# Row maxima of attention: half of the first two key blocks as a relu of differences on ScalarE and one fused add-and-maximum on VectorE

## The chip, the cores and the metric

The kernel runs on one NeuronCore of a Trainium2 chip. Its engines are TensorE (PE in the profile, with its weight loads PEld), VectorE (DVE), ScalarE (ACT), GpSimd (POOL) and SyncE (SP, which only issues DMAs here). The metric is the device time of one execution in microseconds; lower is better. Every engine works through its own instructions in order and waits on semaphores of the others.

## The reference

One transformer block on 2048 rows of width 576, in fp32: a LayerNorm with scale and shift made from a condition `c`, attention with 32 heads of 18 columns, a residual with a gate, a second modulated LayerNorm, and a gated MLP of width 4608.

```python
mod = (_silu(c) @ w_mod).reshape(c.shape[0], 6, 1, -1)
sa, ca, ga, sb, cb, gb = (mod[:, 0], mod[:, 1], mod[:, 2], mod[:, 3], mod[:, 4], mod[:, 5])
h = _layernorm(x, axis=-1) * (1 + ca) + sa
x = x + ga * _A_ref(h, A_wqkv, A_wo)
...
    scores = jnp.einsum("bhqd,bhkd->bhqk", q, k) * scale
    p = _softmax(scores, axis=-1)
    o = jnp.einsum("bhqk,bhkd->bhqd", p, v)
```

The part that matters here is the softmax over 2048 keys, and in it the maximum of each row of scores, which is subtracted before the exponential.

## The kernel before

**Stages.** A first stage makes the modulation, the LayerNorm, and q, k and v; q and k are written to HBM (`qk`) transposed, each as a high part (rounded to PE's fp32r format) and a low part. Then comes attention, and beside its later units the output projection, the second LayerNorm and the operands of the MLP; the MLP follows.

**Units.** Attention runs over 32 units. A unit is one half of the queries (1024) with two heads: units 0 to 15 are the sixteen pairs of heads with the first half, units 16 to 31 the same pairs with the second half. `load_heads(u)` brings a unit's q and k from HBM with eight DMAs on SP's queue, two units ahead; head 0 lies in partitions 0 to 63 and head 1 in 64 to 127, so that matmuls of the two heads lie in different rows of PE. Each head has 54 rows of operands (high times high, high times low, low times high) and two more rows for the negated maximum.

**Maxima.** `maxima()` is a generator that works one unit ahead of the exponentials. A unit has 64 of its turns: for each of 8 query tiles of 128 rows, 4 key blocks of 512 and 2 heads (the head changes fastest, then the key block), one matmul into a PSUM bank (L411) and one VectorE reduce that takes the maximum of the bank's 512 columns into a column of `mx` (L415). At the end of a unit a small reduce (L421) gives the negated maximum `nm` of each row; `spread()` transposes it on PE, splits it into a high and a low part (`mrows`) and sends these by DMA into the spare rows of q. That way the exponentials' matmul subtracts the maximum by itself.

**Steps.** A unit has 16 steps, one per block of 128 keys. In a step, four score matmuls with the keys on the partitions (L877) each give a bank of 128 x 512, each followed by one exponential on ScalarE (L881), and `values()` multiplies the exponentials of two steps earlier with v (L501, eight instructions, in four column groups of PE). The order of PE's instructions is written out by hand: `STEPS` gives one string for even and one for odd steps, where `t` is a score matmul, `m` a turn of the maxima, `v` the values and `w` a place for other work (transposes of outputs and maxima, and in later units a piece of the output projection or of the second LayerNorm). The two steps together make PE's order values, six matmuls, values, ten matmuls. The other engines' order is decided by a scheduler. Maxima are 24 turns and more ahead of the steps, so that the first `m` of a unit is turn 25 of the next unit, that is query tile 3, key block 0, head 1; the eight turns of a query tile thus begin with the last matmul of the group of ten (head 0) and the first one of the group of six (head 1).

**Banks.** `bank()` (L80) hands out seven PSUM banks in turn to maxima, scores and transposes alike; a matmul waits until the bank that was given out seven calls before has been read. The eighth bank, `o`, takes the values of a unit; at its end ScalarE copies it to SBUF (`taken()`, L515), PE transposes it, VectorE takes the reciprocal of the row sums (L529), ScalarE copies the transposed output (L540) and GpSimd scales it (L544).

**Before attention.** `project_qk` multiplies weights and LayerNorm output (L267); ScalarE rounds the high part (L273), VectorE subtracts the low one (L274), and SP's DMA writes them out (L279). In its last part, seven tiles of weights alternate with the first turns of the maxima (`run`). `key_set` sets the spare rows of the key buffers to 1 (L367).

```python
STEPS = "vtmmttmvtm", "tmttwmtmm"
```

Of the kernel before, what the change touches and what calls it, by code (L numbers as in the profile page):

```python
# [15 lines left out]
F32 = mybir.dt.float32  # L16
F32R = mybir.dt.float32r
AF = mybir.ActivationFunctionType
ALU = mybir.AluOpType
# [13 lines left out]
DM = 512  # L33
HALF = D // 2
EPS = 1e-5
SCALE = float(DH) ** -0.5
HW = S // 2
UNITS = H
# [13 lines left out]
def tile_block(ctx, tc, x_in, wqkv, wo, w_gate, w_up, w_down, c_in, w_mod, out):  # L52
# [23 lines left out]
    sc_b = early.tile([P, 5, 32], F32, name="sc_b")  # L76
# [27 lines left out]
    def modulate(row, wm, pieces, takes):  # L104

        pm = bank()
        for parts in pieces:
            for t in range(5):  # L110
                k = ksize(t)
                for v in range(2):
                    for g, to, f0, n in parts:
                        q = 32 * (2 * v + g)
                        nc.tensor.matmul(
                            pm[q : q + 32, to : to + n], sc_b[:k, t, :],
                            wm[t][:k, v * D + f0 : v * D + f0 + n],
                            start=t == 0, stop=t == 4, tile_position=(0, q),
                        )
# [12 lines left out]
        for b in range(3):  # L132
            nc.tensor.transpose(pt[:, b * P : (b + 1) * P], row[:, b * P : (b + 1) * P], ident)
        cols = pt[:, 0:384].rearrange("p (b q) -> p b q", q=P)
        for v, (dst, add) in enumerate(takes):
            if add is None:
                for g in range(2):
                    q = 64 * v + 32 * g
                    nc.sync.dma_start(gates[v : v + 1, g * HALF : (g + 1) * HALF], row[q : q + 1, 0:HALF])
                nc.sync.dma_start(dst, gates[v : v + 1, :].to_broadcast([P, D]))  # L140
            else:
                n = dst.shape[-1]
                nc.vector.tensor_scalar_add(dst[:, 0:3], cols[:, :, 64 * v], add)
                nc.vector.tensor_scalar_add(dst[:, 3:n], cols[:, 0 : n - 3, 64 * v + 32], add)
# [89 lines left out]
    qk = dram.tile([2, 2, D, S], F32R, name="qk")  # L234
# [24 lines left out]
    def project_qk(both, ahead=None):  # L259

        pl = stage.tile([P, 2, 1024], F32R, name="pl")
        for i, ((parts, wh, wl), ch) in enumerate(both):
            acc = bank()
            cols = slice(ch * 512, (ch + 1) * 512)
            ts_ = terms(wh, wl, slice(0, P))
            for n, (w, t) in enumerate(ts_):
                nc.tensor.matmul(  # L267
                    acc, w, hT[:, t, cols], start=n == 0, stop=n == len(ts_) - 1
                )
            if ahead:  # L270
# [3 lines left out]
            nc.vector.tensor_sub(lo, acc, hi.bitcast(F32))  # L274
        for i, ((parts, wh, wl), ch) in enumerate(both):
            p0 = 0
            for col, n in parts:
                which, f0 = col // D, col % D
                nc.sync.dma_start(  # L279
                    qk[which, :, f0 : f0 + n, ch * 512 : (ch + 1) * 512]  # L280
                    .rearrange("l f n -> f l n").bitcast(F32),
                    pl[p0 : p0 + n, :, i * 512 : (i + 1) * 512].bitcast(F32),
                )
                p0 += n

    def load_v(pool, hf):
        raw = pool.tile([P, 5, HALF], F32, name="wv_raw")
# [24 lines left out]
    with tc.tile_pool(name="ln", bufs=2) as ln:  # L312
# [6 lines left out]
        nc.vector.tensor_copy(sc_b, sc.unsqueeze(2).to_broadcast([P, 5, 32]))  # L319

        def normalized(ch):
            xs = []
# [13 lines left out]
        with tc.tile_pool(name="wmp", bufs=1) as wmp:  # L336
            zs = normalized(0)
            wm = wmp.tile([P, 5, 2 * D], F32, name="wm")
            wm = load_mod(wm[:, 0:4, :], wm[:, 4, :], 0)
            modulate(wmp.tile([P, 384], F32, name="mrow"), wm, QUARTERS, [(mcol[:, 1, :], 0.0), (mcol[:, 0, :], 1.0)])  # L340
        nc.gpsimd.memset(vaug, 1.0)
        wts = [load_qk([(0, P)]), load_qk([(D, P)])]
        with tc.tile_pool(name="wv0", bufs=1) as wvp:
            wv = load_v(wvp, 0)
            ln_transpose(ln, zs, hT, 0)
            zs = normalized(1)
            for ch in range(NCH):
# [17 lines left out]
    def key_set(t):  # L365
        for q in (32, 96):
            nc.gpsimd.memset(t[q : q + 32].bitcast(F32), 1.0)  # L367
        return t[:, 0:S]

    ksets = [key_set(temp([P, S], F32R)) for _ in range(2)]  # L370

# [3 lines left out]
    def load_heads(u):  # L375


        qs, ks = heads(u)
        half, p = divmod(u, H // 2)
        own = slice(half * HW, (half + 1) * HW)  # L380
        for h in range(2):
            rows = slice((2 * p + h) * DH, (2 * p + h + 1) * DH)
            two, one = (slice(64 * h + a, 64 * h + b) for a, b in ((0, 2 * DH), (2 * DH, 3 * DH)))
            nc.sync.dma_start(
                qs[two, :].bitcast(F32), qk[0, :, rows, own].rearrange("l f n -> f l n").bitcast(F32)
            )
            nc.sync.dma_start(qs[one, :].bitcast(F32), qk[0, 0, rows, own].bitcast(F32))
# [4 lines left out]
            nc.sync.dma_start(ks[one, :].bitcast(F32), qk[1, 1, rows, :].bitcast(F32))  # L392

    def maxima():

# [2 lines left out]
        last = None  # L398
        for u in range(UNITS):
            qs, ks = heads(u)  # L400
            mx = small.tile([P, 2 * n, 4], F32, name="mx")
            for i in range(8 * n):
                if last is not None and i == (9 if u == 1 else 8):
                    if u == 1:
                        spread(*last)
                    else:
                        state["spread"] = last
                qt, kc, h = i // 8, i // 2 % 4, i % 2
                rows = slice(64 * h, 64 * h + 3 * DH)
                sp = bank()  # L410
                nc.tensor.matmul(  # L411
                    sp, qs[rows, qt * P : (qt + 1) * P],
                    ks[rows, kc * 512 : (kc + 1) * 512], start=True, stop=True,
                )
                nc.vector.tensor_reduce(  # L415
                    mx[:, h * n + qt, kc : kc + 1], sp, axis=AX.X, op=ALU.max
                )
# [12 lines left out]
    def spread(qs, nm):  # L430
# [4 lines left out]
        parts = [small.tile([2 * n, P], F32R, name=f"mrows{l}", bufs=1) for l in range(2)]  # L435
        nc.scalar.copy(parts[0], tp)
        nc.vector.tensor_sub(parts[1], tp, parts[0].bitcast(F32))
        for h in range(2):
# [79 lines left out]
    def outputs():  # L518
# [9 lines left out]
        rec = epool.tile([P, 4, 4], F32, name="rec")  # L528
        nc.vector.reciprocal(rec, tq[:, :, :, DH])  # L529
        if half == 1 and p == H // 2 - 1:  # L530
            state["last"] = epool.tile([P, 8, 2 * DH], F32, name="last")
# [313 lines left out]
    for u in range(UNITS):  # L845
# [6 lines left out]
        for kt in range(NT):  # L852
# [31 lines left out]
            if u in (1, 3):  # L884
                if kt == 2:
# [4 lines left out]
                    row = slots.tile([P, 2560], F32, name="w1")[:, 0:384]  # L890
# [340 lines left out]
```

## Time and profile before

| | before |
|---|---|
| median of three runs | 2932.17 us (2931.83 to 2936.15) |
| span of the profiled execution | 2934.3 us |
| first exponential of attention | 234.76 us from the span's start |
| last exponential ends | near 1598 us |
| PE busy | 2867.2 us (98%) |
| VectorE busy | 2305.1 us (79%) |
| ScalarE busy | 1497.6 us (51%) |
| GpSimd busy | 614.7 us (21%) |

The profile is of one execution. The page gives the span of the program's instructions, and no other time of that execution. Its second part shows the busy share of each engine in 40 slices of 73 us; the fourth to the twenty-second are attention. A group's row holds the line, the engine, the operation, what it writes and reads, the shape, then busy time in us, mean ns of one, and the idle time of the engine just before, with what ended it. In a timeline each row has its start and length in us, with "xN" where instructions in a row are put together, and in brackets the idle time ahead of it. Neighbouring instructions of an engine overlap by some tens of nanoseconds, so that the distance from start to start is shorter than the mean duration. Ends of matmuls are modelled, so "busy" on PE takes in time in which it streams nothing.

### The profile page before, as it was taken

How to read it: one execution, taken by the hardware profiler on the slowest of the kernel's cores; microseconds unless marked ns; L12 is line 12 of the kernel's file. 1: busy time of each engine (PE TensorE's matmuls, PEld its weight loads, DVE VectorE, ACT ScalarE, POOL GpSimd, SP SyncE). 2: the span in 40 equal slices, each digit the busy share in tenths (PEclk: the TensorE clock that was granted, in tenths of full speed). 3: DMA queues.
4: the chain of work that ended last, by engine and by line, in shares of the span. 5: the costliest groups of instructions: out<-in, count | busy, mean ns of one | idle time of the engine just before them, and what ended most of it. 6: DMA issues, size and time to landing. Idle time of an engine off the chain costs nothing.

```text
span 2934.3 us, 46129 instructions
## 1 busy us (share of the span) xinstructions
PE 2867.2 (98%) x17141; PEld 1884.6 (64%) x17141; DVE 2305.1 (79%) x4021; ACT 1497.6 (51%) x2779; POOL 614.7 (21%) x793
## 2 busy tenths in 40 slices
PE   7999999999999999999999999998999999999999
PEld 6974333333334443443443788887888888888888
DVE  7278999999999999999992778888777555555555
ACT  3217778888887678878778333333332111111111
POOL 2001024444213110661102222233221100000000
PEclk9999999999999999999999999999999999999999
DMA  5333113333212110221125866686556854444443
GB/s 170 119 138 115 63 58 134 126 116 112 83 50 70 31 50 19 95 92 60 48 78 185 280 217 231 232 278 242 204 201 225 303 177 168 166 168 169 158 158 137
DMA packets 136089, 420.25 MB, mean 143 GB/s; under 512 B 18805, under 2 KB 56441, under 8 KB 123577
## 3 DMA queue, kind: packets, MB, share of 16 engines
q1 hardware_dynamic: 120472, 338.35, 33.7%
q0 software_dynamic: 15392, 78.95, 7.6%
q8 instruction: 135, 2.21, 0.3%
q14 instruction: 90, 0.73, 0.1%
HBM read 261.13 MB, written 155.59 MB: 142 GB/s over the span
## 4 chain that ended last, share of the span: by engine, by line
PE 85%; DVE 5%; ACT 4%; issue 3%; DMA 2%; SPq 1%; POOL 0%; ACTq 0%; DVEq 0%; POOLq 0%
PE o L501 17%; PE d L1015 14%; PE s L877 13%; PE x L979 13%; PE s L411 9%; PE bg L979 4%; PE bu L979 4%; PE s L267 4%; ACT p L881 3%; PE s L301 2%; PE s L638 2%; DVE w L971 1%; PE s L525 1%; DMA B<-hs 1%; DVE u L1163 0%
## 5 line engine op out<-in xcount | busy, mean ns | idle before, releaser
L415 DVE TENSOR_REDUCE mx<-s 128x1 f32<-128x512 f32 x2048 | 1266.9, 681 | 43.9 <-PE s L411 35.3
L881 ACT ACTIVATE p<-s 128x512 f32<-128x512 f32 x2048 | 1066.9, 607 | 268.7 <-PE s L411 145.4
L411 PE MATMUL s<-k,q 54*128 54x512 f32 x1920 | 658.0, 441 | 2.6 <-ACT p L881 1.0
L877 PE MATMUL s<-q,k 56*128 56x512 f32 x1920 | 581.5, 433 | 6.3 <-ACT p L881 0.4
L877 PEld LDWEIGHTS s<-q,k 56*128 56x128 f32 x1920 | 277.6, 185 | 469.5 <-DVE mx L415 292.6
L501 PE MATMUL o<-p,vaug 128*32 128x512 f32 x4096 | 554.4, 606 | 0.0
L1015 PE MATMUL d<-wd,hh 128*128 128x288 f32 x2304 | 470.9, 298 | 20.9 <-DVE Oa L1019 20.3
L1015 PEld LDWEIGHTS d<-wd,hh 128*128 128x128 f32 x2304 | 375.7, 189 | 35.8 <-DVE Oa L1019 27.2
L411 PEld LDWEIGHTS s<-k,q 54*128 54x128 f32 x1920 | 312.1, 185 | 80.5 <-ACT p L881 37.4
L1019 DVE TENSOR_TENSOR Oa<-Oa,d 128x288 f32<-128x288 f32 x576 | 255.9, 452 | 128.2 <-PE d L1015 123.1
L1015 PE MATMUL d<-wd,hl 128*128 128x288 f32 x1152 | 342.0, 297 | 0.0
L979 PE MATMUL x<-k,w 128*128 128x512 f32 x1008 | 245.5, 394 | 4.7 <-ACT w L970 2.4
L1015 PEld LDWEIGHTS d<-wd,hl 128*128 128x128 f32 x1152 | 218.1, 189 | 0.0
L979 PEld LDWEIGHTS x<-k,w 128*128 128x128 f32 x1008 | 188.8, 190 | 43.2 <-DVE u L1190 3.5
L991 ACT ACTIVATE u<-u 128x512 f32<-128x512 f32 x72 | 45.5, 631 | 318.7 <-DVE u L1179 312.7
L501 PEld LDWEIGHTS o<-p,vaug 128*32 128x32 f32 x4096 | 83.6, 108 | 163.7 <-issue 147.7
L988 ACT ACTIVATE sg<-x 128x512 f32<-128x512 f32 x36 | 21.5, 598 | 309.4 <-PE x L979 309.4
L1021 POOL DMA_DIRECT2D out_dram<-Oa x16 | 8.7, 542 | 606.5 <-DVE Oa L1019 606.5
L979 PE MATMUL x<-big,w 128*128 128x512 f32 x504 | 120.6, 390 | 1.0 <-issue 1.0
L979 PE MATMUL x<-w,w 128*128 128x512 f32 x504 | 121.0, 390 | 0.0
L267 PE MATMUL s<-hT,wq_h 128*128 128x512 f32 x324 | 106.1, 399 | 1.9 <-DVE hT L204 1.2
L979 PEld LDWEIGHTS x<-big,w 128*128 128x128 f32 x504 | 94.3, 188 | 21.0 <-issue 1.4
(221 smaller groups left out, 3345.2 us busy)
## 6 DMA issues: line engine op xcount, KB each, us to landing
ws<-w SPq DMA_DIRECT2D x126, 640.0 KB
w<-ws SPq DMA_DIRECT2D x126, 640.0 KB
wd<-wds SPq DMA_DIRECT2D x36, 1152.0 KB
wds<-w POOLq DMA_DIRECT2D x18, 1152.0 KB, 4.5
k<-qk SPq DMA_DIRECT2D x60, 288.0 KB
qk<-pl SPq DMA_DIRECT2D x32, 512.0 KB
w<-in_B_w_down_dram POOLq DMA_DIRECT2D x18, 576.0 KB, 4.9
q<-qk SPq DMA_DIRECT2D x64, 144.0 KB
```

The costliest lines, as they stand in the source:

```text
L267: nc.tensor.matmul(acc, w, hT[:, t, cols], start=n == 0, stop=n == len(ts_) - 1)
L301: nc.tensor.matmul(acc[:, 0:HALF], hT[:, k, rows], w, start=n == 0, stop=n == len(ts_) - 1,)
L411: nc.tensor.matmul(sp, qs[rows, qt * P : (qt + 1) * P], ks[rows, kc * 512 : (kc + 1) * 512], start=True, stop=True,)
L415: nc.vector.tensor_reduce(mx[:, h * n + qt, kc : kc + 1], sp, axis=AX.X, op=ALU.max)
L501: nc.tensor.matmul(acc[32 * j : 32 * j + 32, :], vaug[:, kt, (2 * p + h) * VW : (2 * p + h) * VW + 32], probs[2 * c + h], start=kt == 0, s ...
L638: nc.tensor.matmul(acc[:, :HALF], a, w, start=i == 0, stop=i == len(ts_) - 1)
L877: nc.tensor.matmul(sT, ks[rows, kcols], qs[rows, c * 512 : (c + 1) * 512], start=True, stop=True)
L881: state["exp"] = nc.scalar.activation(pr, sT, AF.Exp, scale=SCALE)
L979: nc.tensor.matmul(acc[v], w[:, v, a, :], X[s][:, b, :], start=first and n == 0, stop=n == 6, skip_group_check=not first,)
L991: nc.scalar.activation(t[:, 0:512], t[:, 0:512], AF.Sigmoid)
L1015: nc.tensor.matmul(acc[:, :HALF], a[:, f, rows], w[:, f, cols], start=n == 0, stop=n == 5)
L1019: nc.vector.tensor_add(Oa[:, t, cols], Oa[:, t, cols], acc[:, :HALF])
```

## The change

For the maximum of two numbers, max(a, b) = b + relu(a - b). The change uses it for key blocks 0 and 1 of one head in each query tile (head 0 in even tiles, head 1 in odd ones), in units 2 to 31. For these pairs the matmul of key block 0 takes a fifth block of key columns in place of block 0, which holds the differences between keys 0 to 511 and keys 512 to 1023, so that it gives a - b. ScalarE writes its relu to an SBUF tile (`over`). When the matmul of key block 1 has given b, one VectorE instruction adds both and takes the maximum over the columns into column 0 of `mx`; it is followed by a read of the accumulator. Column 1 of these rows of `mx` stays at a lowest value that GpSimd writes once. The number of matmuls does not change.

The differences are made while k is projected (`key_differences`): five GpSimd instructions on 128 x 512 (or 64 x 512) elements and one DMA on GpSimd's queue, for five groups of key rows: one in the first stage, one in each of the three later tiles with 128 rows of k, and one in the last tile, which has 64. HBM's `qk` becomes `qd` and `kd`, with 2560 columns of keys; `load_heads` loads all of them from unit 2 on. To make room in SBUF, the modulation's broadcast operand `sc_b` is rebuilt in each modulation, the two `mrows` tiles become one, `last` takes the place of `oT`, and `mx` becomes two fixed tiles.

```diff
+        sc_b = row[:, 384:544].rearrange("p (t c) -> p t c", c=32)
+        nc.vector.tensor_copy(sc_b, sc.unsqueeze(2).to_broadcast([P, 5, 32]))
+        row = row[:, 0:384]
...
+    def key_differences(pool, a, b, p0, n, f0):
+        rows = slice(p0, p0 + n)
+        a, b = a[rows].bitcast(F32), b[rows].bitcast(F32)
+        d = pool.tile([P, 512], F32, name="kd_d")[rows]
+        e = pool.tile([P, 512], F32, name="kd_e")[rows]
+        parts = pool.tile([P, 2, 512], F32R, name="kd_p")[rows]
+        nc.gpsimd.tensor_sub(d, a[:, 0, :], b[:, 0, :])
+        nc.gpsimd.tensor_sub(e, a[:, 1, :], b[:, 1, :])
+        nc.gpsimd.tensor_add(d, d, e)
+        nc.gpsimd.tensor_copy(parts[:, 0, :], d)
+        nc.gpsimd.tensor_sub(parts[:, 1, :], d, parts[:, 0, :].bitcast(F32))
+        nc.gpsimd.dma_start(
+            kd[:, f0 : f0 + n, S : S + 512].rearrange("l f n -> f l n").bitcast(F32), parts.bitcast(F32)
+        )
...
             for ch in range(NCH):
-                project_qk([(wt, ch) for wt in wts])
+                pls.append(project_qk([(wt, ch) for wt in wts]))
+                if ch == 1:
+                    key_differences(wvp, pls[0][:, :, 512:1024], pls[1][:, :, 512:1024], 0, P, 0)
...
+        n = S if u < 2 else S + 512
...
-                ks[two, :].bitcast(F32),
-                qk[1, 0, rows, :].unsqueeze(1).to_broadcast([DH, 2, S]).bitcast(F32),
+                ks[two, 0:n].bitcast(F32),
+                kd[0, rows, 0:n].unsqueeze(1).to_broadcast([DH, 2, n]).bitcast(F32),
...
+            if u in (2, 3):
+                nc.gpsimd.memset(mx[:, :, 1], LOWEST)
...
+                paired = u >= 2 and h == qt % 2 and kc < 2
+                at = NCH if paired and kc == 0 else kc
                 sp = bank()
                 nc.tensor.matmul(
                     sp, qs[rows, qt * P : (qt + 1) * P],
-                    ks[rows, kc * 512 : (kc + 1) * 512], start=True, stop=True,
+                    ks[rows, at * 512 : (at + 1) * 512], start=True, stop=True,
                 )
-                nc.vector.tensor_reduce(
-                    mx[:, h * n + qt, kc : kc + 1], sp, axis=AX.X, op=ALU.max
-                )
+                to = mx[:, h * n + qt, kc : kc + 1]
+                if not paired:
+                    nc.vector.tensor_reduce(to, sp, axis=AX.X, op=ALU.max)
+                elif kc == 0:
+                    over = small.tile([P, 512], F32, name="over", bufs=1)
+                    nc.scalar.activation(over, sp, AF.Relu)
+                else:
+                    nc.vector.tensor_tensor_reduce(
+                        out=over, in0=sp, in1=over, scale=1.0, scalar=LOWEST,
+                        op0=ALU.add, op1=ALU.max, accum_out=mx[:, h * n + qt, 0:1],
+                    )
...
             for g in range(2):
-                project_qk([(wt, 2 * g), (wt, 2 * g + 1)], run if i else None)
+                pl = project_qk([(wt, 2 * g), (wt, 2 * g + 1)], run if i else None)
+                col, n = parts[-1]
+                if g == 0 and col >= D:
+                    key_differences(wvp, pl[:, :, 0:512], pl[:, :, 512:1024], P - n, n, col - D)
```

More of the change, by code (lines that the diff above doesn't have):

```diff
@@ L35 @@
 EPS = 1e-5
+LOWEST = -3.4e38
 SCALE = float(DH) ** -0.5
@@ L75, in tile_block @@
     sc = early.tile([P, 5], F32, name="sc")
-    sc_b = early.tile([P, 5, 32], F32, name="sc_b")
     turns = {"s": 0, "to": 65 + 4 * LEAD, "bank": 0}
@@ L233, in tile_block @@
     xs = dram.tile([2, 7, P, 5, 512], F32R, name="xs")
-    qk = dram.tile([2, 2, D, S], F32R, name="qk")
+    qd = dram.tile([2, D, S], F32R, name="qd")
+    kd = dram.tile([2, D, S + 512], F32R, name="kd")
     wds = dram.tile([NB, P, 4 * D], F32R, name="wds")
@@ L279, in project_qk @@
                 nc.sync.dma_start(
-                    qk[which, :, f0 : f0 + n, ch * 512 : (ch + 1) * 512]
+                    (qd, kd)[which][:, f0 : f0 + n, ch * 512 : (ch + 1) * 512]
                     .rearrange("l f n -> f l n").bitcast(F32),
@@ L339, in tile_block @@
             wm = load_mod(wm[:, 0:4, :], wm[:, 4, :], 0)
-            modulate(wmp.tile([P, 384], F32, name="mrow"), wm, QUARTERS, [(mcol[:, 1, :], 0.0), (mcol[:, 0, :], 1.0)])
+            modulate(wmp.tile([P, 544], F32, name="mrow"), wm, QUARTERS, [(mcol[:, 1, :], 0.0), (mcol[:, 0, :], 1.0)])
         nc.gpsimd.memset(vaug, 1.0)
@@ L367, in key_set @@
             nc.gpsimd.memset(t[q : q + 32].bitcast(F32), 1.0)
-        return t[:, 0:S]
+        return t
     ksets = [key_set(temp([P, S], F32R)) for _ in range(2)]
@@ L384, in load_heads @@
             nc.sync.dma_start(
-                qs[two, :].bitcast(F32), qk[0, :, rows, own].rearrange("l f n -> f l n").bitcast(F32)
+                qs[two, :].bitcast(F32), qd[:, rows, own].rearrange("l f n -> f l n").bitcast(F32)
             )
-            nc.sync.dma_start(qs[one, :].bitcast(F32), qk[0, 0, rows, own].bitcast(F32))
+            nc.sync.dma_start(qs[one, :].bitcast(F32), qd[0, rows, own].bitcast(F32))
             nc.sync.dma_start(
-                ks[two, :].bitcast(F32),
-                qk[1, 0, rows, :].unsqueeze(1).to_broadcast([DH, 2, S]).bitcast(F32),
-            )
-            nc.sync.dma_start(ks[one, :].bitcast(F32), qk[1, 1, rows, :].bitcast(F32))
+                ks[two, 0:n].bitcast(F32),
+                kd[0, rows, 0:n].unsqueeze(1).to_broadcast([DH, 2, n]).bitcast(F32),
+            )
+            nc.sync.dma_start(ks[one, 0:n].bitcast(F32), kd[1, rows, 0:n].bitcast(F32))
+    mxs = [small.tile([P, 2 * HW // P, 4], F32, name=f"mx{i}", bufs=1) for i in range(2)]
     def maxima():
@@ L400, in maxima @@
             qs, ks = heads(u)
-            mx = small.tile([P, 2 * n, 4], F32, name="mx")
+            mx = mxs[u % 2]
+            if u in (2, 3):
+                nc.gpsimd.memset(mx[:, :, 1], LOWEST)
             for i in range(8 * n):
@@ L434, in spread @@
         nc.tensor.transpose(tp, nm.rearrange("p h t -> p (h t)"), ident)
-        parts = [small.tile([2 * n, P], F32R, name=f"mrows{l}", bufs=1) for l in range(2)]
+        mrows = small.tile([32 + 2 * n, P], F32R, name="mrows", bufs=1)
+        parts = [mrows[32 * l : 32 * l + 2 * n] for l in range(2)]
         nc.scalar.copy(parts[0], tp)
@@ L530, in outputs @@
         if half == 1 and p == H // 2 - 1:
-            state["last"] = epool.tile([P, 8, 2 * DH], F32, name="last")
+            state["last"] = epool.tile([P, 512], F32, name="oT")[:, 0 : 16 * DH].rearrange("p (t e) -> p t e", t=8)
             for h in range(2):
@@ L889, in tile_block @@
                     mods = load_mod(a, b, 1 + u // 2)
-                    row = slots.tile([P, 2560], F32, name="w1")[:, 0:384]
+                    row = slots.tile([P, 2560], F32, name="w1")[:, 0:544]
                 elif kt == 10 and u == 1:
```

3 lines of the change are left out of this document (2 added, 1 removed).

## The prediction

> **What bounds the kernel now.** I read the page first (slices, costliest groups), then the table by stretches, then timelines of single engines inside one unit, because the first two views point at different engines.
>
> ```profile
> DVE  7278999999999999999992778888777555555555
> L415 DVE TENSOR_REDUCE mx<-s 128x1 f32<-128x512 f32 x2048 | 1266.9, 681 | 43.9 <-PE s L411 35.3
> L881 ACT ACTIVATE p<-s 128x512 f32<-128x512 f32 x2048 | 1066.9, 607 | 268.7 <-PE s L411 145.4
> L411 PE MATMUL s<-k,q 54*128 54x512 f32 x1920 | 658.0, 441 | 2.6 <-ACT p L881 1.0
> L877 PEld LDWEIGHTS s<-q,k 56*128 56x128 f32 x1920 | 277.6, 185 | 469.5 <-DVE mx L415 292.6
> ```
>
> On this page attention looks bound by VectorE: it is 90% busy or more for twenty slices, nearly all of it in the maxima (L415), and PE's weight loads are said to wait 292.6 us for those. A change that takes maxima off VectorE should then pay. But the idle time before L415 was ended by PE, so VectorE also waits. Which of the two sets the pace is seen inside a unit (columns: stretch, its length, then busy us and instructions of PE, weight loads, DVE, ACT, POOL):
>
> ```profile
> 652.00:692.90 40.90, 40.55 (x265) 16.20 (x261) 40.13 (x69) 34.04 (x68) 18.68 (x30) 1.00 0.36 122
> 990.90:1039.60 48.70, 48.57 (x329) 23.61 (x327) 44.39 (x82) 34.49 (x68) 8.33 (x17) 1.00 0.12 39
> 1563.70:1598.00 34.30, 34.28 (x199) 11.11 (x199) 0.26 (x1) 33.25 (x67) 4.00 (x7) 1.00 0.40 137
> ```
>
> These are an ordinary unit (40.9 us), one that shares PE with the output projection (48.7) and the last one, without maxima (34.3, ScalarE-bound). A unit is eight periods of two steps. One period, from its values (L501) to the same values of the next, in the timeline of the weight loads:
>
> ```profile
> 635.11 0.16 PEld L501 LDWEIGHTS o<-p,vaug 128*32 128x32 f32 x8 [0.25 <-issue]
> 636.11 0.18 PEld L877 LDWEIGHTS s<-q,k 56*128 56x128 f32 x1 [0.84 <-DVE mx L415]
> 637.01 0.16 PEld L501 LDWEIGHTS o<-p,vaug 128*32 128x32 f32 x8 [0.37 <-issue]
> 638.01 0.18 PEld L877 LDWEIGHTS s<-q,k 56*128 56x128 f32 x1 [0.84 <-DVE mx L415]
> 639.25 0.18 PEld L877 LDWEIGHTS s<-q,k 56*128 56x128 f32 x1 [0.46 <-ACT p L881]
> 639.74 0.18 PEld L411 LDWEIGHTS s<-k,q 54*128 54x128 f32 x1 [0.19 <-ACT p L881]
> 640.16 0.16 PEld L501 LDWEIGHTS o<-p,vaug 128*32 128x32 f32 x8 [0.24 <-issue]
> ```
>
> and in the last unit, where VectorE does nothing:
>
> ```profile
> 1578.16 0.53 PEld L877 LDWEIGHTS s<-q,k 56*128 56x128 f32 x5 [0.84 <-issue]
> ```
>
> The 0.84 after each values group stands there too, with no maximum left to wait for. So it is the values' own matmuls, and the 292.6 us put down to L415 are a label on time that PE spends working. PE's real waits in a period are the 0.46 and the 0.19, and both end on an exponential. ScalarE and VectorE in the same period:
>
> ```profile
> 636.70 1.58 ACT L881 ACTIVATE p<-s 128x512 f32<-128x512 f32 x3 [0.60 <-PE s L411]
> 638.60 2.07 ACT L881 ACTIVATE p<-s 128x512 f32<-128x512 f32 x4 [0.33 <-PE s L411]
> 636.52 0.21 DVE L421 TENSOR_REDUCE nm<-mx 128x16 f32<-128x64 f32 x1
> ```
>
> The loop is this. PE: values 1.00 (635.11 to 636.11), a short group of six matmuls 0.90, values 1.00, a long group of ten 2.15 (638.01 to 640.16): 5.05 in all. In the long group the score matmul at 638.01 is followed by its exponential at 638.60 (0.60 long), and only then can the score at 639.25 go out: the two are seven banks apart in a ring of seven. That is a PE-ScalarE loop without VectorE. This period also holds the nm reduce, work that VectorE doesn't have in the others, and it is no longer: 8 periods of 5.05 are 40.4, and I put the rest of 40.9 down to the few transposes of a unit. So I hold that VectorE is nearly as long as the loop, but is not it.
>
> **The change part by part.** *Maxima* (30 units, 8 pairs each: 240). Two reduces go, one fused instruction with an accumulator read comes (in the built program: 480 reduces fewer, 240 and 240 more), and ScalarE gets 240 relus.
>
> ```profile
> 225.38 2.48 DVE L415 TENSOR_REDUCE mx<-s 128x1 f32<-128x512 f32 x4 [0.96 <-PE s L411]
> L1179 DVE TENSOR_TENSOR u<-x,u 128x512 f32<-128x512 f32 x72 | 49.6, 691 | 67.7 <-PE x L979 67.6
> L971 DVE TENSOR_TENSOR w<-raw,w 128x512 fp32r<-128x512 f32 x54 | 53.1, 984 | 0.3 <-DMA wd<-wds 0.2
> L437 DVE TENSOR_TENSOR mrows<-s,mrows 16x128 fp32r<-16x128 f32 x32 | 8.9, 278 | 19.7 <-ACT mrows L436 19.4 <-DMA ga_b<-gates 0.3
> ```
>
> A reduce costs (2.48-0.68)/3 = 0.60 from start to start. The fused one has no row. Its main part is bounded by L1179 (PSUM and SBUF in, 0.69) and the slowest two-input row of that size (0.98), its read by 0 and the 0.28 of a small instruction: 0.61 to 1.26 with 0.08 of overlap taken off below. I take 0.82 (0.69+0.21-0.08), since L1179 has the same operands. A pair then saves 2 x 0.60 - 0.82 = 0.38, a unit 3.0 us of VectorE. All of it lies beside the loop above: gain 0. If the cover is gone (VectorE bound after all), it is the first rival.
>
> The fused instruction waits for its relu, with the rest of VectorE's queue behind it. For head 0 the pair straddles a values group, and its relu runs in ScalarE's 0.60 of idle time before 636.70: free. For head 1 the built program's ScalarE order is exp, relu, exp, exp, exp. A step of ScalarE is (2.07-0.62)/3 = 0.48. The three exps from 636.70 leave it free at 636.70+3 x 0.48 = 638.14; with the relu at 638.62, against 638.60 now. So the loop moves by 0.02, four periods a unit: 0.1 us. The fused one starts at relu's end, 636.70+0.48+0.60 = 637.8. Next on VectorE is the maximum whose matmul goes out at 638.01 with the score; its bank is wanted again seven banks later, at about 639.6, so its reduce (0.68) has to start by 638.85. The fused one may thus take 1.0 before PE feels it.
>
> In the first period of every unit that slack is already used, by the copy of the last unit's output:
>
> ```profile
> 652.03 1.58 ACT L881 ACTIVATE p<-s 128x512 f32<-128x512 f32 x3 [0.60 <-PE s L877]
> 653.52 0.59 ACT L515 COPY oT<-o 128x512 f32<-128x512 f32 x1
> 654.00 1.09 ACT L881 ACTIVATE p<-s 128x512 f32<-128x512 f32 x2
> 655.58 0.16 PEld L501 LDWEIGHTS o<-p,vaug 128*32 128x32 f32 x8 [0.25 <-PE s L411]
> 650.43 0.16 PEld L501 LDWEIGHTS o<-p,vaug 128*32 128x32 f32 x8 [0.24 <-issue]
> ```
>
> That period is 5.15, a tenth longer, as the exponential of the long group comes at 654.00 instead of 653.9. The built order there is exp, relu, exp, exp, copy, exp, in every unit, since the period always falls on a head 1 pair. So the copy moves to 653.95, the exponential to 654.43, and the score behind it, PE's order and the next values by 0.43. Thirty units have this; in nine (16 to 20, 27 to 30, where PE has the projection's matmuls to do meanwhile: the 48.7 above) I count it as hidden. 21 x 0.43 = 9.0, plus 2 for the 0.1 per unit: **+11**. From 0 (all hidden) to 15 (nothing hidden).
>
> *Key differences* (five groups of five POOL instructions and one DMA on POOL's queue). Three run in a stretch where POOL is idle; the first, behind which the copies of the next LayerNorm queue, and its reads beside VectorE's, I price at 0 to 2, taking 0.5. The last one ends late: its buffers lie where the probabilities go, and in the built order ScalarE's table load for the first exponential waits for its DMA.
>
> ```profile
> 227.78 0.68 DVE L274 TENSOR_TENSOR pl<-s,pl 128x512 fp32r<-128x512 f32 x1
> 233.47 1.28 ACT L881 ACT_TABLE_LOAD   x1
> L613 POOL TENSOR_TENSOR t<-t,t 128x512 fp32r<-128x512 f32 x8 | 10.2, 1279 | 0.7
> L679 POOL CAST t<-t 128x512 fp32r<-128x512 f32 x14 | 8.5, 608 | 0.3 <-DMA xs<-t 0.2
> xs<-t POOLq DMA_DIRECT2D x5, 256.0 KB, 2.9
> L367 POOL MEMSET k<- 32x2560 f32 x6 | 13.4, 2227 | 156.3 <-DMA qk<-pl 156.0
> ```
>
> Its second subtraction needs the low part, ready at 228.46. Then 1.28+1.28+0.61+1.28 and the DMA's 2.9: 235.8, with semaphores 236.2. The table load now starts at 233.47, so **+2.7** (0.5 if 64 partitions take half the time, 4.5 with a slow DMA). Behind it all of attention shifts; the key memsets, queued behind the DMA on POOL, waited until later anyway.
>
> *The rest* is priced at nothing: key loads a quarter larger (eight DMAs a unit as before; 2.6 us is all that L411 ever waited), mrows in one tile, `sc_b` rebuilt by one small VectorE copy a modulation (placed many reduces ahead of its use; 0.3 us each if not), two memsets on POOL. Table loads are as many as before.
>
> Sum: 11 + 0.5 + 2.7 = **+14 us** on the profiled execution's span of 2934.3, which lies 2.1 above the median of 2932.17 (the page gives no other time of it): about **2946**.
>
> **The rivals.** *VectorE is the bound (faster).* For it: 40.13 busy of 40.90. Then a unit falls to what ScalarE allows, 34.04 + 8 x 0.48 = 37.9, plus the last unit's 1.05 of pauses 38.9; halfway 38.4, 2.5 less in some 20 units: -50, +3 at the start: 2885. Against it: the nm period and the 0.84 of the last unit.
>
> *Nothing (no change).* The copy may go ahead of the exps' lateness, or PE's order absorb it: then +0 to +5, 2935.
>
> *A slow fused instruction (much slower).* If it is longer than 1.0, the bank of the next maximum comes free late and PE stalls in the long group in each period: at 1.26 by some 0.25, 8 x 0.25 x 21 = 42 more, 2988. For it: two 128x512 inputs took 0.98 elsewhere. Against: those rows have both in SBUF.
> The Trainium skill, "Vector Engine (DVE) Microarchitecture Reference", section "Points that are easy to get wrong", says that the scalar-tensor-tensor shape of instruction halves its throughput with two non-bf16 SBUF sources; here one source is PSUM, so by its letter it doesn't apply, and no row here shows it.
> If it ran at half rate, the slope between L1179 and the row below, (691-452)/224 = 1.07 ns an element, adds 0.55: 1.37, a stall of some 0.35, +59, 3005.
>
> ```profile
> L1019 DVE TENSOR_TENSOR Oa<-Oa,d 128x288 f32<-128x288 f32 x576 | 255.9, 452 | 128.2 <-PE d L1015 123.1
> ```
>
> **How the numbers follow.** My case (2939 to 2965) 0.56, slow fused instruction 0.13 (half rate 0.04 of it), no change 0.17, faster 0.14. A difference under 0.2% (5.9 us) can't be told from none. Faster 0.14, same 0.17, slower 0.69. The range 2928 to 2990 leaves out the faster case and the worst half of the slow one.
>
> **What would show it.** Right: ordinary units of 41.3 to 41.5, the first period 5.5 to 5.6 and the others 5.05 to 5.1; VectorE's busy time down by 3 us a unit with new idle time that PE ends; the first exponential near 237.5. Wrong: ordinary units under 40.5 (VectorE was the bound), all eight periods longer (fused instruction or relu late), a changed time outside attention.

## The result, and the profile after

The changed kernel takes 2947.48 us (median of four runs, 2943.52 to 2950.31) against 2932.43 for the kernel before on the same chip: ratio 1.0046, 95% interval 1.0032 to 1.0061. Six more runs later, beside runs of the kernel before on the same chip, gave 2946.27 against 2933.88, ratio 1.0039 (1.0025 to 1.0053). So it is slower by 0.4%, 12 to 15 us, where 14 were predicted. The two profiles alone show less, 2934.3 to 2941.7, since the profiled run of before was the longest of its runs listed and the profiled run of after the shortest of its four.

The page of the changed kernel (VectorE's slices, then the groups that answer to those shown of before, then the two new ones):

```profile
DVE  7278888888888888998882777788777555555555
L923 ACT ACTIVATE p<-s 128x512 f32<-128x512 f32 x2048 | 1072.2, 615 | 170.3 <-PE s L441 118.0
L447 DVE TENSOR_REDUCE mx<-s 128x1 f32<-128x512 f32 x1568 | 1007.9, 685 | 131.0 <-PE s L441 87.1
L441 PE MATMUL s<-k,q 54*128 54x512 f32 x1920 | 642.9, 440 | 2.0 <-ACT p L923 2.0
L919 PEld LDWEIGHTS s<-q,k 56*128 56x128 f32 x1920 | 294.2, 185 | 497.0 <-ACT p L923 238.8
L452 DVE CUSTOM_DVE_ANT_0 over<-s,over 128x512 f32<-128x512 f32 x240 | 164.7, 686 | 23.0 <-ACT over L450 21.8
L450 ACT ACTIVATE over<-s 128x512 f32<-128x512 f32 x240 | 148.4, 618 | 0.0
```

VectorE went from nines to eights, it is idle for 131 us ahead of its reduces in place of 44, most of it ended by PE, and the kernel became no shorter. The weight loads show how little the label of a wait can mean: idle for 469.5 us before with 292.6 put down to VectorE's maxima, idle for 497.0 after with 238.8 put down to ScalarE. In both, 402 us of it are the 479 waits of 0.84 behind values groups, which are the values' own matmuls; before, 290.9 of the 292.6 are among them. The fused instruction waited 21.8 us in all for its relu, 0.09 each.

An ordinary unit, one beside the output projection, and the last, in the table by stretches (stretch, length, busy us and instructions of PE, weight loads, DVE, ACT, POOL):

```profile
657.90:699.20 41.30, 41.06 (x265) 16.59 (x261) 36.47 (x68) 37.59 (x76) 18.70 (x30) 1.00 0.37 127
998.80:1047.10 48.30, 48.08 (x329) 23.41 (x328) 40.83 (x82) 38.03 (x75) 8.37 (x17) 1.00 0.15 45
1573.10:1607.30 34.20, 34.15 (x197) 10.98 (x193) 0.26 (x1) 33.15 (x67) 4.02 (x7) 1.00 0.41 139
```

Against 40.9, 48.7 and 34.3: VectorE gave 3.7 us a unit (40.13 to 36.47), and the ordinary unit grew by 0.4. The unit beside the projection is 0.4 shorter, which was not foreseen.

The first period of that ordinary unit, in ScalarE's timeline, and its two ends in that of the weight loads:

```profile
657.93 0.60 ACT L923 ACTIVATE p<-s 128x512 f32<-128x512 f32 x1 [0.59 <-PE s L441]
658.43 0.59 ACT L450 ACTIVATE over<-s 128x512 f32<-128x512 f32 x1
658.90 1.10 ACT L923 ACTIVATE p<-s 128x512 f32<-128x512 f32 x2
659.86 0.62 ACT L557 COPY oT<-o 128x512 f32<-128x512 f32 x1
660.33 2.61 ACT L923 ACTIVATE p<-s 128x512 f32<-128x512 f32 x5
```

```profile
656.34 0.16 PEld L543 LDWEIGHTS o<-p,vaug 128*32 128x32 f32 x8 [0.24 <-issue]
661.03 0.18 PEld L919 LDWEIGHTS s<-q,k 56*128 56x128 f32 x1 [0.68 <-ACT p L923]
661.95 0.16 PEld L543 LDWEIGHTS o<-p,vaug 128*32 128x32 f32 x8 [0.25 <-PE s L441]
```

Here is the queue that was predicted: exponential, relu, two exponentials, copy, exponential, without a gap. The period is 661.95 - 656.34 = 5.61, where it was 5.15 before.

The start, in ScalarE's timeline of before (the last cast of the projections, the table load, the first exponentials) and, in the second block, of after:

```profile
232.86 0.59 ACT L273 CAST pl<-s 128x512 fp32r<-128x512 f32 x1 [3.27 <-PE s L267]
233.47 1.28 ACT L881 ACT_TABLE_LOAD   x1
234.76 1.57 ACT L881 ACTIVATE p<-s 128x512 f32<-128x512 f32 x3
```

```profile
231.64 0.59 ACT L277 CAST pl<-s 128x512 fp32r<-128x512 f32 x1 [3.21 <-PE s L271]
235.58 1.28 ACT L923 ACT_TABLE_LOAD   x1 [3.35 <-DMA kd<-kd_p]
236.88 4.03 ACT L923 ACTIVATE p<-s 128x512 f32<-128x512 f32 x8
```

The table load stood right behind the cast and now waits 3.35 us for the DMA of the last differences. From cast to first exponential it is 5.24 in place of 1.90. That the first exponential is only 2.1 later by the clock is chance: the first cast of the projections falls at 30.2 to 34.5 us in the first nine profiles taken, two of them of kernels whose code up to there is unchanged, and it was early here (30.2) and 32.2 in the profile of before.

### The profile page after: what moved, and what is told of

The parts are those of the page before. It is cut to its first block, busy times and chain, and to the rows that moved or that the text cites. A ratio compares the mean times of both kernels' runs of the same rounds, so it can differ in the third digit from the quotient of the medians.

```text
span 2941.7 us, 46621 instructions
## 1 busy us (share of the span) xinstructions
PE 2873.2 (98%) x17141; PEld 1891.5 (64%) x17141; DVE 2205.7 (75%) x4023; ACT 1604.0 (55%) x3019; POOL 648.8 (22%) x825
## 4 chain that ended last, share of the span: by engine, by line
PE 84%; DVE 5%; DMA 3%; issue 3%; ACT 3%; POOL 1%; SPq 1%; DVEq 0%; POOLq 0%; ACTq 0%
PE o L543 16%; PE d L1057 14%; PE s L919 13%; PE x L1021 12%; PE s L441 10%; PE bu L1021 4%; PE bg L1021 4%; PE s L271 4%; PE s L322 2%; PE s L680 2%; ACT p L923 1%; DVE w L1013 1%; DMA ws<-w 1%; PE s L567 1%; DMA B<-hs 1%
## 5 line engine op out<-in xcount | busy, mean ns | idle before, releaser
L447 DVE TENSOR_REDUCE mx<-s 128x1 f32<-128x512 f32 x1568 | 1007.9, 685 | 131.0 <-PE s L441 87.1
L441 PE MATMUL s<-k,q 54*128 54x512 f32 x1920 | 642.9, 440 | 2.0 <-ACT p L923 2.0
L919 PE MATMUL s<-q,k 56*128 56x512 f32 x1920 | 613.3, 439 | 4.8 <-ACT p L923 4.8
L919 PEld LDWEIGHTS s<-q,k 56*128 56x128 f32 x1920 | 294.2, 185 | 497.0 <-ACT p L923 238.8
L441 PEld LDWEIGHTS s<-k,q 54*128 54x128 f32 x1920 | 305.9, 185 | 60.7 <-ACT p L923 34.1
L452 DVE CUSTOM_DVE_ANT_0 over<-s,over 128x512 f32<-128x512 f32 x240 | 164.7, 686 | 23.0 <-ACT over L450 21.8
L450 ACT ACTIVATE over<-s 128x512 f32<-128x512 f32 x240 | 148.4, 618 | 0.0
```

Source lines behind the costliest of these rows:

```text
L441: nc.tensor.matmul(sp, qs[rows, qt * P : (qt + 1) * P], ks[rows, at * 512 : (at + 1) * 512], start=True, stop=True,)
L447: nc.vector.tensor_reduce(to, sp, axis=AX.X, op=ALU.max)
L450: nc.scalar.activation(over, sp, AF.Relu)
L452: nc.vector.tensor_tensor_reduce(out=over, in0=sp, in1=over, scale=1.0, scalar=LOWEST, op0=ALU.add, op1=ALU.max, accum_out=mx[:, h * n + q ...
L919: nc.tensor.matmul(sT, ks[rows, kcols], qs[rows, c * 512 : (c + 1) * 512], start=True, stop=True)
```

## Experiments

Three explanations were kept apart. *Collision*, the prediction's: units are longer where a relu and the copy of oT stand ahead of one exponential. *Bulk*: ScalarE's 3.6 us more a unit cost wherever they stand. *VectorE*: it sets the pace after all, and its relief is eaten by something. A fourth, *second waits*, came out of the first runs. This table has what the traces of all kernels gave; an ordinary unit is the median of units 4 to 15, counted from first exponential to first exponential, and the last column is the ratio to the kernel before on the same chip.

| kernel | cast to first exponential | ordinary unit | unit 18 (projection) | attention | median us | ratio (95%) |
|---|---|---|---|---|---|---|
| before | 1.90 | 40.87 | 48.73 | 1363.3 | 2932.4 | |
| changed | 5.24 | 41.27 | 48.32 | 1370.4 | 2947.5 | 1.0046 (1.0032-1.0061) |
| changed, again | 5.21 | 41.27 | 48.32 | 1370.1 | 2946.3 | 1.0039 (1.0025-1.0053) |
| fourth tile plain | 5.21 | 40.79 | 48.14 | 1361.4 | 2936.4 | 1.0008 (0.9999-1.0016) |
| copy of oT on VectorE | 5.24 | 40.76 | 48.36 | 1361.7 | 2939.3 | 1.0019 (1.0011-1.0028) |
| all pairs on head 0 | 5.22 | 40.59 | 47.61 | 1352.2 | 2928.3 | 0.9980 (0.9972-0.9989) |
| all pairs on head 1 | 5.21 | 41.73 | 49.09 | 1386.8 | 2963.2 (1 run) | |
| no pairs | 5.23 | 40.91 | 48.71 | 1365.5 | 2943.8 | 1.0036 (1.0022-1.0049) |
| before + tiny copy | 1.90 | 40.59 | 48.66 | 1359.7 | 2928.1 | 0.9985 (0.9976-0.9994) |
| head 0 + filler | 5.26 | 41.31 | 49.57 | 1382.9 | 2958.7 | 1.0084 (1.0068-1.0099) |
| early buffer | 1.90 | 41.27 | 48.31 | 1371.7 | 2942.5 | 1.0031 (1.0021-1.0041) |
| head 0 + early buffer | 1.90 | 40.57 | 47.65 | 1353.5 | 2922.7 | 0.9970 (0.9960-0.9979) |
| the same, again | 1.90 | 40.57 | 47.62 | 1352.0 | 2925.2 | 0.9963 (0.9951-0.9976) |
| the same + copy of oT on VectorE | 1.90 | 40.57 | 48.07 | 1355.9 | 2929.3 | 0.9980 (0.9971-0.9989) |

**Where the relu stands.** Three edits of the changed kernel:

```
all pairs on head 0:    paired = u >= 2 and h == 0 and kc < 2
fourth tile plain:      paired = u >= 2 and h == qt % 2 and kc < 2 and qt != 3
copy of oT on VectorE:  nc.vector.tensor_copy(oT, acc)      # was nc.scalar.copy
```

All pairs on head 0:

> All 240 pairs stay, but every one is a head 0 pair, also in the first period of a unit; same relus and fused instructions in number. Collision theory (a head 1 relu and the copy of oT stand ahead of one exponential in the first period): the first period falls from 5.61 to about 5.15, ordinary units from 41.26 to 40.9 or less (the head 0 periods of the changed kernel are 0.07 shorter than those of before, so down to 40.4), about 8 to 15 us less than the changed kernel, 2932 to 2940. Rival, bulk: 3.6 us a unit more on ScalarE or the wait of the fused instruction for its relu (21.8 in all) costs wherever the relu stands: units stay at 41.2 to 41.3, 2947. Rival, VectorE: its work is the same as in the changed kernel, so no change either.

Fourth tile plain:

> The fourth query tile of each unit, the one whose pair falls beside the copy of oT, has two plain maxima again; 210 pairs instead of 240, VectorE gets 30 x 0.4 us more. Collision theory: first period back to 5.15, ordinary units 41.26 to about 40.85, 8 to 12 us less than the changed kernel: 2935 to 2940. Bulk rival: an eighth of 0.4 a unit comes back, 1 to 2 us: 2945. VectorE rival: more work for VectorE, so 0 to 12 us slower than the changed kernel.

Copy of oT on VectorE:

> The changed kernel with the copy of oT on VectorE, which has 4 us to spare a unit. Collision theory: the first period falls from 5.61 to 5.05 to 5.15, ordinary units from 41.26 to 40.7 to 40.8, 10 to 15 us less than the changed kernel: 2932 to 2938. Bulk rival: ScalarE is 0.6 us a unit lighter of 37.6, at most 0.06 us a unit: 2945 to 2947. VectorE rival: 0.6 us a unit more on the engine that sets the pace, 10 us or more slower.

Ordinary units, in the tables by stretches of the three:

```profile
653.30:693.90 40.60, 40.45 (x265) 16.28 (x261) 35.91 (x68) 37.92 (x76) 18.70 (x30) 1.00 0.36 125
```

```profile
657.00:697.80 40.80, 40.67 (x265) 16.49 (x261) 36.83 (x68) 37.09 (x75) 18.70 (x30) 1.00 0.36 127
```

```profile
655.90:696.70 40.80, 40.80 (x265) 16.52 (x261) 36.84 (x69) 37.09 (x75) 18.71 (x30) 1.00 0.37 127
```

All three bring the first period from 5.61 to 5.12 to 5.16 and the unit down by 0.5 to 0.7. Times are near what was expected: 4 us under the collision's range with head 0 pairs, inside it with the plain tile, 1 over it with the copy moved. Bulk falls: with all pairs on head 0 ScalarE is as busy as in the changed kernel (37.9 against 37.6 us) and the unit is shorter than before the change. VectorE falls as what sets ordinary units: a copy of 0.69 was added to it and the unit got shorter. The collision stands. But head 0 pairs went 0.3 a unit below the 40.9 that the collision alone gives, and the kernel with them is faster than the one before. In the period tables a plain period is 5.05, one with a head 0 pair 4.99 and one with a head 1 pair 5.11.

**Second waits.** The 0.06 of head 0 periods lies between a score's weight load and its exponential, at the start of the long group. Before, from the timelines of the weight loads and of ScalarE:

```profile
668.75 0.18 PEld L877 LDWEIGHTS s<-q,k 56*128 56x128 f32 x1 [0.84 <-DVE mx L415]
```

```profile
669.35 2.06 ACT L881 ACTIVATE p<-s 128x512 f32<-128x512 f32 x4 [0.33 <-PE s L877]
```

and with all pairs on head 0:

```profile
669.95 0.18 PEld L919 LDWEIGHTS s<-q,k 56*128 56x128 f32 x1 [0.84 <-ACT p L923]
```

```profile
670.48 2.06 ACT L923 ACTIVATE p<-s 128x512 f32<-128x512 f32 x4 [0.26 <-PE s L441]
```

0.60 against 0.53. The traces also record the semaphores that these two exponentials wait for (the fourth exponential of a period in both). With head 0 pairs it waits for PE's alone. Before, the exponential waits for ScalarE's own semaphore, for a write that stands eleven or more ScalarE instructions earlier in the built program and was done long ago, and the wait for PE stands in an extra semaphore instruction on ScalarE's queue at 669.289, 0.06 ahead of the exponential at 669.350. Over all groups between 280 and 1560 us in which ScalarE was free, the median distance from weight load to exponential is 0.594 where there are two waits (204 long groups and 125 short ones of before) and 0.533 or 0.534 where there is one (207 long groups with head 0 pairs, 111 short ones of before). The 2048 exponentials carry 1033 such extra instructions before and 795 after: where the relu stands in the queue decides which exponentials are left with one. The Trainium skill, "Perfetto Trace Analysis", section "Identifying Dependency Chains", says that an instruction that waits for several engines may get extra semaphore instructions ahead of it. The trace agrees, though here the second semaphore is the engine's own. The extra instruction costs 0.06 where the engine is idle.

To test this without pairs, the kernel before got one tiny ScalarE copy per tile at the place of a head 0 relu, ahead of the reduce:

```
...
+                if h == 0 and kc == 0:
+                    nc.scalar.copy(tick[:, 1:2], sp[:, 0:1])
                 nc.vector.tensor_reduce(
...
```

> The kernel before (no differences, no pairs, all 2048 reduces) with one tiny ScalarE copy (128x1, from the maximum's bank into a scratch tile that nobody reads) in each query tile where a head 0 relu stands. Two-wait theory: an exponential that waits for a second semaphore, ScalarE's own, starts 0.06 later (0.594 against 0.533 after its score's weight load in the traces so far); in the built program the copy takes these second waits off the first exponential of both groups. Periods of 4.93 to 4.99, ordinary units 40.87 to 40.0 to 40.5, 10 to 25 us faster than the kernel before, with VectorE's work as before. Rival (head 0 periods are 0.06 shorter since VectorE is lighter there): units at 40.9 to 41.0, 0 to 5 us slower than before.

Its ordinary unit, and the long group's first score and exponential:

```profile
652.40:693.00 40.60, 40.48 (x263) 16.55 (x263) 39.50 (x68) 34.51 (x75) 18.69 (x30) 1.00 0.35 122
```

```profile
674.14 0.18 PEld L882 LDWEIGHTS s<-q,k 56*128 56x128 f32 x1 [0.84 <-DVE mx L420]
```

```profile
674.68 2.06 ACT L886 ACTIVATE p<-s 128x512 f32<-128x512 f32 x4 [0.32 <-PE s L414]
```

0.54, periods of 4.99, units of 40.59: all of the gain of head 0 pairs in ordinary units, with VectorE's work as before (39.5 us in place of 40.1, since one reduce fewer falls into this stretch) and 1033 extra instructions down to 415. So that gain is not relief of VectorE. The unit is just over the 40.0 to 40.5 expected, and the time fell by 4.7 us, less than the 10 to 25: the short group's exponential came earlier too (0.53), but PE did not wait for it there.

**How much VectorE has to spare.** All pairs on head 0, with an idle reduce behind each fused instruction:

```
+                    nc.vector.tensor_reduce(to, sp[:, 0:320], axis=AX.X, op=ALU.max)
```

> All pairs on head 0, and behind each fused instruction a reduce of 320 columns of the same bank (its result changes nothing), so that VectorE has as much to do as before the change, some 40 us a unit. Two-wait theory, VectorE only cover: ordinary units as with head 0 pairs alone, 40.55 to 40.65, time within 3 us of that kernel. VectorE rival: units back to 40.87 or more, 5 to 10 us slower than head 0 pairs alone.

```profile
660.80:702.10 41.30, 41.30 (x265) 16.65 (x261) 38.20 (x76) 37.99 (x76) 18.71 (x30) 1.00 0.37 126
```

```profile
666.49 0.68 DVE L452 CUSTOM_DVE_ANT_0 over<-s,over 128x512 f32<-128x512 f32 x1
667.09 0.08 DVE L452 DVE_READ_ACCUMULATOR2_ANT mx<- 128x1 f32 x1
667.09 0.49 DVE L456 TENSOR_REDUCE mx<-s 128x1 f32<-128x320 f32 x1
667.50 1.88 DVE L447 TENSOR_REDUCE mx<-s 128x1 f32<-128x512 f32 x3
```

The two-wait expectation failed. The unit went where the VectorE rival put it (40.87 or more), but the time is 30 us over that of head 0 pairs alone, where the rival gave 5 to 10. With less VectorE work than before the change (38.2 us against 40.1) the unit is longer, 41.3. Two of its eight periods grew from 5.23 to 5.53 and a third from 4.99 to 5.13; the others are as without the filler. So not the amount of VectorE's work counts here but how late it is at one place: fused instruction and filler take 667.50 - 666.49 = 1.01 in place of 0.60. In the weight loads of that period, the last maximum of the long group now waits for a bank that VectorE has still to read:

```profile
669.43 0.18 PEld L441 LDWEIGHTS s<-k,q 54*128 54x128 f32 x1 [0.25 <-DVE mx L447]
```

With head 0 pairs alone the same load does not wait (0.06 of idle time); both hold in all of units 4 to 15. The limit of 1.0 in the prediction was worked out for a head 1 pair; for head 0 it gave none.

**The other side, and the parts alone.** All pairs on head 1 (`h == 1` in the condition), and the changed kernel without pairs (`paired = False`):

> All 240 pairs on head 1, one look. Theory: a head 1 pair's relu makes its period 5.11 where a plain one is 5.05 and a head 0 one 4.99, and 5.61 beside the copy of oT; so ordinary units of 41.24 + 4 x 0.09 = 41.6 (41.5 to 41.8). Bulk rival (place doesn't matter): 41.26.

> The changed kernel with the pairs taken out: key differences are still made, stored and loaded with the keys, but every maximum is a plain reduce; no relu, no fused instruction. If pairs alone lengthen the units: ordinary units back to 40.85 to 40.9, first exponential still late (237 to 239.5 against 234.8), time 2 to 5 us over the kernel before. Rival, the larger key loads and the POOL work cost inside attention too: ordinary units of 40.95 or more, and 5 to 15 us over the kernel before.

In the weight loads of a head 1 period away from the copy:

```profile
683.10 0.18 PEld L919 LDWEIGHTS s<-q,k 56*128 56x128 f32 x1 [0.29 <-ACT p L923]
683.58 0.18 PEld L919 LDWEIGHTS s<-q,k 56*128 56x128 f32 x1 [0.19 <-ACT p L923]
684.08 0.18 PEld L441 LDWEIGHTS s<-k,q 54*128 54x128 f32 x1 [0.20 <-ACT p L923]
```

Three waits for exponentials in place of two: the relu among the short group's exponentials delays the banks that the long group wants. Units of 41.73 met the 41.6 expected. Without pairs the units are back at 40.9, and the larger key loads cost at most 0.04 a unit. Its time, 10.9 over before (interval 6.5 to 14.4), missed the 2 to 5 expected and is more than the new work accounts for in its profile: 3.3 at the table load, 0.6 in the projections and 2.2 in attention make 6.1. In that profile the first cast is 2.3 late as well, by chance, and the profiled run of before (2936.15) lies 3.3 above the median that it is compared with (2932.85); how much of this belongs to the change stays open.

**The start.** The parts of the last four groups of differences in the buffer of unit 2's queries, in the changed kernel and then with all pairs on head 0:

```
...
-        parts = pool.tile([P, 2, 512], F32R, name="kd_p")[rows]
+        parts = (pool.tile([P, 2, 512], F32R, name="kd_p") if parts is None else parts)[rows]
...
+                        qsets[2].rearrange("p (l n) -> p l n", l=2),
...
```

> The changed kernel with only the buffer of the last four groups of differences moved to unit 2's queries; the pairs as changed. Gate theory: table load right behind the last cast, first exponential 3.3 us earlier counted from that cast, time 3 to 4 us under the changed kernel beside it. If the gate's time is taken up behind it (key memsets, loads of unit 0 and 1): 0 to 1 us.

> All pairs on head 0, and the two parts of the last four groups of key differences stand in the buffer of unit 2's queries, not where the probabilities go. If it is the DMA of the last group that holds ScalarE's table load: first exponential from 237.7 back to 234.8 to 235.5, 2 to 3 us less than head 0 pairs alone, so 0.25 to 0.3% under the kernel before. If something else holds it, the first exponential stays at 237 or later and the time is that of head 0 pairs alone.

The early buffer in the changed kernel:

```profile
232.66 0.59 ACT L277 CAST pl<-s 128x512 fp32r<-128x512 f32 x1 [3.21 <-PE s L271]
233.27 1.28 ACT L926 ACT_TABLE_LOAD   x1
234.56 1.58 ACT L926 ACTIVATE p<-s 128x512 f32<-128x512 f32 x3
```

The wait is gone, 1.90 from cast to exponential as before the change, and the time 3.8 us under the changed kernel beside it. With all pairs on head 0 this is the fastest kernel of the study.

**Repeats, and one step further.** The changed kernel again, the fastest again, and the fastest with the copy of oT on VectorE:

> The changed kernel itself, more runs of it beside the next two. Theory: +4 at the start (0.7 in the projections, 3.3 by which the first exponential waits for the last group's DMA) and +5 to +7 in the units, so a median 9 to 12 us over the kernel before. If its first four runs (15 over) were typical: 13 to 17.

> Head 0 pairs and early differences again, on the chip of the kernel above, for the comparison: 2920 to 2926, 0.25 to 0.35% under the kernel before.

> Head 0 pairs and early differences as in the fastest kernel so far, and the copy of oT on VectorE besides, which has 4.7 us a unit to spare there. Two-wait and collision theory: the first period falls from 5.14 to 4.99, ordinary units from 40.57 to 40.42, 3 to 4 us less than that kernel. Against it: VectorE is late just behind a fused instruction, and 0.69 more at that place may make the next maximum late (the filler's two longer periods): the first period 5.14 or longer, no gain or up to 10 us more.

The changed kernel is 12.4 over before again, between the two ranges that were given. The fastest kernel held: 2925.15 against 2933.38 (ratio 0.9963, 0.9951 to 0.9976). The copy on VectorE made it 4.1 slower: 2929.29 (0.9980, 0.9971 to 0.9989). The first period stayed at 5.15, units at 40.57, and those beside the projection grew from 47.6 to 48.1.

In the first period one wait took the place of another. With the copy on ScalarE, a score of the long group waits for the exponential that the copy delays:

```profile
694.33 0.18 PEld L922 LDWEIGHTS s<-q,k 56*128 56x128 f32 x1 [0.53 <-ACT p L926]
```

With the copy on VectorE this wait is 0.38, as in the other periods, but the next maximum waits for a bank whose reduce stands behind the copy on VectorE:

```profile
695.65 0.18 PEld L922 LDWEIGHTS s<-q,k 56*128 56x128 f32 x1 [0.38 <-ACT p L926]
696.28 0.19 PEld L441 LDWEIGHTS s<-k,q 54*128 54x128 f32 x2 [0.45 <-DVE mx L447]
```

```profile
694.95 0.68 DVE L560 COPY oT<-o 128x512 f32<-128x512 f32 x1
695.54 1.88 DVE L447 TENSOR_REDUCE mx<-s 128x1 f32<-128x512 f32 x3
```

These waits are the same in all of units 5 to 15. It is what the expectation had against the edit: VectorE has time to spare in the unit, but not at this place.

## Why the prediction was right

**The bound.** PE and ScalarE set the period of ordinary units, as argued from the 0.84 after the values and the two waits for exponentials. VectorE gave 3.7 us a unit (3.0 predicted) for no gain. The sign given for the contrary, units under 40.5, was not reached even with head 0 pairs, and the kernel with the tiny copy shows that their 40.59 is no work of VectorE. Units 17 to 19 are the exception: they are 0.4 shorter after and 1.1 with head 0 pairs, and no shorter without pairs. VectorE was 44.4 us busy of 48.7 there. That they follow VectorE's load (the filler makes them 49.6) fits the first rival in those three units, 1.3 us in all; but with all pairs on head 1, and the same load, they are 49.1, so this is not shown. The direct test, the kernel before with each maximum taken over half of its columns, gave no time, since a value was no longer finite without the other keys.

**The fused instruction.** From 0.61 to 1.26 was allowed, 0.82 taken. It was the lower end: start to start 667.09 - 666.49 = 0.60, its read hidden in the next reduce. The slow rival is out. The halved throughput that the Trainium skill ("Vector Engine (DVE) Microarchitecture Reference", section "Points that are easy to get wrong") gives for two non-bf16 SBUF sources did not appear with one source in PSUM: the mean is 686 ns.

**The relu.** Head 0 free: it was better than free, by 0.06 a period, through second waits that the prediction did not look at. Head 1: 0.02 a period predicted, 0.06 measured, as a third wait of PE. The two nearly cancel in the changed kernel, which pairs both heads in turn.

**The first period.** 0.43 predicted, 0.46 measured (5.15 to 5.61), and three edits that part relu and copy take it away. The chain behind it, copy, exponential, score, next values, was right; with the copy on VectorE the score's wait is shorter, 0.38 in place of 0.53.

**The sum.** Attention grew by 7.1 us (1363.3 to 1370.4), where 11 were predicted. Units 0 to 15 grew by 6.2, close to what was counted for them; 16 to 20, counted as hidden, lost 0.6; 21 to 26, where six times 0.43 was counted, lost 0.4; 27 to 30, counted as hidden, took 1.9, of which unit 28 alone 1.3. The start cost 3.4 to 4.1 where 3.2 were predicted: 3.3 at the table load (2.7), and 0.1 to 0.8 in the projections from first cast to last (0.5), 200.65 to 201.43 where the granted clock up to there was 0.985 and 200.34 (the kernel with the tiny copy) to 200.48 where it was 0.993. The traces thus account for 11, the medians say 12 to 15; that the total came near the predicted 14 is partly luck, as the units were overestimated by 4.

As far as the runs show, the last 1 to 4 us go with the granted clock, which the prediction did not consider. Single runs of the kernel before lie between 2928.6 and 2943.6, and their medians fall with the clock: 2940.6 at 0.992 (4 runs), 2936.8 at 0.993 (13), 2933.8 at 0.994 (24), 2932.2 at 0.995 (28), 2929.9 at 0.996 (12). The ten runs of the changed kernel had 0.993 on average, the kernel before 0.994. At the same clock the changed kernel's medians are 2949.2 at 0.992 (4), 2945.5 at 0.993 (3), 2946.8 at 0.994 (2) and 2943.5 at 0.995 (1), so 9 to 13 over. Why it was granted the lower clock is not shown.

## What to carry to other kernels

Work moved to an idle engine is free only at a place in its queue where it was idle: the same 240 relus made this kernel 0.2% faster or 1% slower (a single run), by which of two heads they served. So read the queue around the move for what already fills its slack (here a copy once a unit; with head 0 pairs its period was as long with it on VectorE as on ScalarE), and hold a wait's label against a stage where the named engine does nothing. A buffer that shares memory with the next stage ties that stage to the last DMA that reads it; another home for it was worth 3.3 us.

## What the runs showed of the hardware that was not expected

An exponential on an idle ScalarE that has a second semaphore to wait for starts 0.06 us later than one with a single wait (0.594 against 0.533 after its score's weight load), though the second had long been met; taken off the exponentials at the head of a group, that was worth 0.3 us a unit of 40.9. The fused add and maximum of a PSUM and an SBUF operand, 128x512 f32, costs VectorE 0.60 us from start to start, as a plain reduce of one operand does, and its accumulator read of 0.08 us lies wholly beside the next instruction.
